# Score chunks made seven ahead from the second block on, and turned-score stores, x stores and v loads issued by GpSimd

## The chip, the cores and the metric

The kernel runs on one core of one Trainium2 chip. The metric is the device time of one execution in microseconds (us), the median of several runs.

## What is computed

Three layers follow each other; B = 4, S = 3072, D = 256, and the inner width of z is 64.

```python
scores = (1.0 / S) * np.matmul(z, z.transpose(0, 2, 1))
attn = np.maximum(scores, 0.0) ** 2
x = u * np.matmul(attn, v)

x_prev = np.concatenate([np.zeros((B, 1, D)), x[:, :-1, :]], axis=1)
xk = mu_k * x + (1.0 - mu_k) * x_prev
xr = mu_r * x + (1.0 - mu_r) * x_prev
k = np.maximum(xk @ w_k, 0.0)
x = 1.0 / (1.0 + np.exp(-(xr @ w_r))) * (k * k @ w_v)

g = np.maximum(x.reshape(B * S, D) @ w_in, 0.0) ** 2
return g @ w_out
```

The change touches the first layer alone, the attention. Its scores are symmetric, since both factors are z.

## The kernel before

The attention of a batch is cut into 6 blocks of 512 queries, 24 blocks in all, numbered here from 0; block `ib` of a batch has 24 **steps**, one for each 128 keys. A step's **chunk** is the 128x512 piece of the squared scores that it needs, split into a high and a low part (`ahi`, `alo`) so that two float32r products stand for one of float32. `attend` (line 406) multiplies the chunk's parts by v's parts (`vhl`), 12 matmuls a step.

A chunk comes about in one of two ways, both in `scores`. For key groups `g >= ib` (a group is 4 chunks) it is computed: six matmuls for two chunks (line 374), relu and square on ScalarE (lines 357 and 378), the high part on ScalarE or VectorE (lines 383 and 381), the low part on VectorE (line 388). For `g > ib` VectorE also turns it (line 335) into a staging tile `turn`, of which there are two; when the group's fourth chunk is in it, the tile is stored to DRAM (`turned`, 1 MB; line 342 in one DMA, or line 340 in four). For `g < ib` the chunk is not computed: the turned piece, stored by an earlier block of the same batch, is loaded into a tile `mixed` (lines 351 and 353) and split (lines 366 and 367).

The program is written in a fixed order, and each engine runs its share in that order. The loop at the end of `attention` goes over the steps. At each it first runs what `at_step` has put there (loads of z, u, v, the turned pieces; the splitting of v and z), then makes the chunks up to step + `ahead`, then does the step's `attend`. `ahead` is 4 in blocks 0 to 2, 5 in block 3, 6 in block 4 and 7 from block 5 on, and it is 0 at a block's steps 21 and 22, in every block, so that no chunk is made there; the chunks left out are made at step 23, behind the block's `gate`. The gate (lines 413 to 429) takes the sums out of PSUM on ScalarE and VectorE, multiplies by u and stores x to DRAM. The next block's sums take the same PSUM banks.

All DMAs but four are issued by SyncE (SP), one after the other; an issue whose wait is not over holds up those behind it. v's loads stand on line 94 (one DMA for a group) or line 288 (four DMAs, groups 2 to 4), eight steps ahead of their splitting. z's second half is copied from its first by a DMA (line 270), which `prep_z` issues 7 steps after z's load; ScalarE takes the high part of the result (line 277) 4 steps after that.

Of the kernel before, what the change touches and what calls it, by code (L numbers as in the profile page):

```python
# [15 lines left out]
P = 128  # L16
Q = 32
T = 512
# [3 lines left out]
def tile_relu2_attention__rwkv_channel_mix__relu2_mlp(  # L22
# [18 lines left out]
    nc = tc.nc  # L41
    B, S, D = u.shape
# [4 lines left out]
    NJ = S // P  # L47
# [7 lines left out]
    G = 4  # L55
# [21 lines left out]
    xT = [dram.tile([D, S], F32, name=f"xT{b}") for b in range(B)]  # L77
    R = P // Q
# [10 lines left out]

    raws = {}  # L90

    def load_raw(key, src, n, w):
        t = raw_p.tile([P, n, w], src.dtype, tag="raw", name="raw")
        nc.sync.dma_start(out=t, in_=src)
        raws[key] = t

    def split_raw(key, hi, lo):
# [139 lines left out]
    def load_piece(i):  # L237
        if i < len(w_pieces):
            src = w_pieces[i][0]
            load_raw(("w32", i), src, src.shape[1], src.shape[2])  # L240

    def attention():
        with ExitStack() as st:
# [3 lines left out]
            FIRST, LEAD = 4, 7  # L247
# [33 lines left out]
            def load_v(b, g):  # L281
                src = v[b, g * T:(g + 1) * T, :]
                if g not in apart:
                    load_raw(("v", b, g), src.rearrange("(c p) d -> p c d", p=P), G, D)
                    return
                raws["v", b, g] = t = raw_p.tile([P, G, D], F32, tag="raw", name="raw")
                for k in range(R):
                    nc.sync.dma_start(out=t[k * Q:(k + 1) * Q], in_=src.rearrange("(r c k) d -> k r c d", r=Q, k=R)[k])

            def hold_v(b, g):  # L290
                vhl[b, g] = zp.tile([P, 2, G, D], F32R, tag="vhl", name="vhl", bufs=NG)
# [39 lines left out]
            def turn(a, i, j, c):  # L331
                if c == 0:
                    staged[i, j] = io.tile([P, R, G, G, Q], F32, tag="turn", name="turn")
                t, s = staged[i, j], spread[i, j]
                nc.vector.transpose(t[:, :, :, c, :], a.rearrange("x (m q r) -> x q m r", m=G, q=R))  # L335
                if c == G - 1:
                    to, src = turned[i, j], t.rearrange("x q m c k -> x q (m c k)")
                    if s:
                        for p in range(R):
                            nc.sync.dma_start(out=to[p].rearrange("q r f -> r q f"), in_=src[p * Q:(p + 1) * Q])  # L340
                    else:
                        nc.sync.dma_start(out=to.rearrange("q x f -> x q f"), in_=src)

            def load_turned_scores(n, g, k):

# [44 lines left out]
            def finish(f=None):  # L390

                if late:
                    late.pop()()
                if f:
                    late.append(f)
# [13 lines left out]
            def gate(n, d):  # L409
                b, t0 = n // NB, (n % NB) * T  # L410
                o, halves = uT.pop((n, d)), acc.pop((n, d))
                part = x_tile[:, d, 0:T] if n < NBLK - 2 else pools["cv"].tile([P, T], F32, tag="em"[d], name="part")
                nc.scalar.copy(part, halves[1])
                if d == 0:
                    rest = io.tile([P, T], F32, tag="rest", name="rest", bufs=1)
                    nc.scalar.copy(rest, halves[0])  # L416
                    spare[n] = rest, part
                    gates.append(lambda: nc.vector.tensor_tensor(out=part, in0=rest, in1=part, op=ALU.add))
                else:
                    nc.vector.tensor_tensor(out=part, in0=halves[0], in1=part, op=ALU.add)  # L420

                def end():
                    to, t_in, u_in = o, part, o
                    if n % NB in apart:
                        to = spare[n][d]
                        t_in, u_in = (t.rearrange("x (k r) -> x k r", r=Q) for t in (t_in, u_in))
                    nc.vector.tensor_tensor(out=to if to is o else to.rearrange("x (r k) -> x k r", r=Q),
                                            in0=t_in, in1=u_in, op=ALU.mult)
                    nc.sync.dma_start(out=xT[b][d * P:(d + 1) * P, t0:t0 + T], in_=to)

                gates.append(end)

# [3 lines left out]
            def at_step(s, f, *a):  # L436
                todo.setdefault(s, []).append((f, a))
# [3 lines left out]
            for n in range(NBLK - 1):  # L441
                b, ib = divmod(n, NB)
                for g in range(ib):
                    need, stored = n * NJ + (g + ib // (NB - 1)) * G - LEAD, (b * NB + g) * NJ + ib * G + G - 1 - FIRST
                    s = max(need - EARLY, stored + 1, freed[-3] if len(freed) > 2 else 0, taken)
                    d = min(3, (need - 3 - s) // 4) or 0.5
# [8 lines left out]
            for b in range(1, B):  # L455
                end = b * NB * NJ
                for g in range(NG):
                    s = end + NJ * (g // 2 - 3) + 6 + 9 * (g % 2)
                    at_step(s, load_z, b, g)
                    for k in range(3):  # L460
                        at_step(s + (7, 11, 13)[k], prep_z, b, g, k)
                    s = end - NJ + G * ((g + 1) % NG) + 5
                    at_step(s - 8, load_v, b, g)
                    for h in range(2):
                        for lo in range(2):
                            at_step(s + 2 * h + lo, prep_v, b, g, h, lo)
# [13 lines left out]
            for n in range(NBLK):  # L480
                s = n * NJ
# [14 lines left out]
            for i, (src, done, rests) in enumerate(conversions):  # L496
                b = i * B // len(conversions)
# [19 lines left out]
            s = n_steps - NJ  # L517
# [11 lines left out]
            for s in range(-FIRST, n_steps + 1):  # L529
                for f, a in todo.pop(s, ()):  # L530
                    f(*a)
                if made == n_steps:
                    finish()
                j = s % NJ if 0 <= s < n_steps else None
                if j in (1, NJ - 1):
                    attend(s, 0, range(3))
                    if j > 1:
                        gate(s // NJ, 0)
                    attend(s - 1, 1, range(3))
                    at.pop(s - 1)  # L540
                    if j > 1:
                        attend(s, 1, range(3))
                        at.pop(s)
                        gate(s // NJ, 1)
                        while gates:
                            gates.pop(0)()
                ahead = 0 if j in (NJ - 3, NJ - 2) else min(LEAD, FIRST + max(0, s - 2 * NJ) // NJ)
                while made < min(n_steps, s + 1 + ahead):
                    scores(made)
                    made += 1  # L550
                if j in (0, NJ - 2):
                    attend(s, 0, range(3))
                elif j == 1:
                    attend(s, 1, range(3))
                    at.pop(s)
                elif j is not None and j < NJ - 2:
                    for d, terms in ((0, (0, 1)), (1, (0, 1)), (0, (2,)), (1, (2,))):
                        attend(s, d, terms)
                    at.pop(s)
# [385 lines left out]
```

## Time and profile before

| what | us |
|---|---|
| median of 3 runs (2543.63 to 2548.68) | 2547.32 |
| the profiled execution, its own time | 2547.61 |
| its span in the profile | 2545.8 |
| attention, to the end of block 23, about | 969 |
| the two layers after it, about | 1577 |

The profile is of one execution. A block of the attention ends, for this document, where VectorE's instruction of line 420 ends; the stretches of the rows below are cut there. The engines are PE (matmul), PEld (weight load), DVE (VectorE), ACT (ScalarE), POOL (GpSimd) and SP, whose issues are marked SPq. "Idle before" names what ended an engine's idle time. A DMA's landing is the time from its issue to its completion.

### The profile page before, as it was taken

The numbers are of one execution on the slowest core, as the hardware profiler recorded it, in microseconds if no ns is written. First come the engines' busy times: TensorE is split into PE (matmuls) and PEld (weight loads), VectorE is DVE, ScalarE is ACT, GpSimd is POOL, SyncE is SP. The second block draws the span as 40 slices with busy tenths as digits, with TensorE's granted clock in tenths as the row PEclk, the third lists the DMA queues.
The fourth block names the chain that finished last, engine by engine and source line by source line (L and its number), as shares of the span: only waits on it lengthen the run. The fifth ranks groups of instructions, "written<-read, shape, count | busy, mean of one in ns | idle before, by whom it ended". The sixth has DMA issues, their size and how long they took to land.

```text
span 2545.8 us, 39407 instructions
## 1 busy us (share of the span) xinstructions
PE 2495.3 (98%) x14832; PEld 2061.4 (81%) x14832; DVE 1988.6 (78%) x3390; ACT 1685.1 (66%) x2943; POOL 0.2 (0%) x4
## 2 busy tenths in 40 slices
PE   7999999999999999999999999999999999999998
PEld 5787788778878878888888888788888888888887
DVE  7777787798878876888888877777777777777776
ACT  7776786697778755555655555666666666666665
POOL 0000000000000000000000000000000000000000
PEclk9999999999999999999999999999999999999999
DMA  8567758767777761212222112011110011010100
GB/s 203 150 165 196 190 160 201 185 189 192 181 194 203 172 176 61 83 63 84 82 71 87 42 67 67 18 26 25 34 34 17 18 34 34 22 29 18 34 17 17
DMA packets 304528, 244.30 MB, mean 96 GB/s; under 512 B 194385, under 2 KB 212817, under 8 KB 304337
## 3 DMA queue, kind: packets, MB, share of 16 engines
q1 hardware_dynamic: 302224, 241.39, 36.1%
q8 instruction: 116, 1.90, 0.3%
q10 hardware_dynamic: 2112, 0.39, 0.1%
q14 instruction: 76, 0.61, 0.1%
HBM read 134.50 MB, written 104.86 MB: 94 GB/s over the span
## 4 chain that ended last, share of the span: by engine, by line
PE 87%; DVE 4%; ACT 3%; DMA 2%; SPq 2%; issue 1%; DVEq 0%; ACTq 0%
PE v L406 25%; PE ups L733 16%; PE ups L208 13%; PE v L749 6%; PE v L750 6%; PE v L751 6%; PE sps L374 4%; PE v L234 3%; PE v L230 3%; PE v L231 3%; DMA mixed<-turned 1%; ACT a L357 1%; ACT a L378 1%; SPq L255 1%; SPq L351 1%
## 5 line engine op out<-in xcount | busy, mean ns | idle before, releaser
L406 PE MATMUL v<-ahi,vhl 64*128 64x512 f32 x4608 | 675.4, 391 | 6.8 <-ACT rest L416 5.5
L406 PEld LDWEIGHTS v<-ahi,vhl 64*128 64x128 f32 x4608 | 472.7, 186 | 97.4 <-ACT rest L416 10.7
L406 PE MATMUL v<-alo,vhl 64*128 64x512 f32 x2304 | 414.0, 392 | 26.0 <-DVE alo L367 18.9
L770 ACT ACTIVATE s<-s 128x512 f32<-128x512 f32 x288 | 181.3, 629 | 333.0 <-DVE s L765 332.9
L733 PE MATMUL ups<-d,win 128*128 128x512 f32 x1152 | 323.6, 389 | 0.0
L406 PEld LDWEIGHTS v<-alo,vhl 64*128 64x128 f32 x2304 | 250.4, 186 | 74.1 <-DVE alo L367 21.9
L749 PE MATMUL v<-hhi,wout 128*128 128x512 f32 x768 | 299.3, 390 | 1.0 <-ACT hhi L778 0.8
L751 PE MATMUL v<-hlo,wout 128*128 128x512 f32 x768 | 299.3, 390 | 0.4 <-DVE hlo L784 0.4
L750 PE MATMUL v<-hhi,wout 128*128 128x512 f32 x768 | 298.8, 389 | 0.0
L208 PE MATMUL ups<-mixed,wk 128*128 128x512 f32 x1152 | 291.8, 389 | 0.0
L784 DVE TENSOR_TENSOR hlo<-s,hhi 128x512 fp32r<-128x512 f32 x384 | 264.6, 689 | 22.2 <-ACT hhi L778 10.8
L160 ACT ACTIVATE a<-ups 128x512 f32<-128x512 f32 x192 | 115.1, 600 | 238.3 <-PE ups L208 231.5
L733 PEld LDWEIGHTS ups<-d,win 128*128 128x128 f32 x1152 | 216.3, 188 | 44.9
L208 PEld LDWEIGHTS ups<-mixed,wk 128*128 128x128 f32 x1152 | 216.2, 188 | 44.9
L733 PE MATMUL ups<-b,win 128*128 128x512 f32 x864 | 242.9, 389 | 0.0
L773 ACT ACTIVATE s<-s 128x512 f32<-128x512 f32 x384 | 231.6, 628 | 6.1
L357 ACT ACTIVATE a<-sps 128x512 f32<-128x512 f32 x336 | 198.6, 591 | 40.3 <-PE sps L374 36.8
L388 DVE TENSOR_TENSOR alo<-a,ahi 128x512 fp32r<-128x512 f32 x336 | 221.0, 661 | 0.0
L378 ACT ACTIVATE a<-a 128x512 f32<-128x512 f32 x336 | 213.1, 634 | 10.2
L335 DVE STREAM_TRANSPOSE turn<-a 128x512 f32<-128x512 f32 x240 | 169.4, 706 | 40.5 <-ACT a L378 35.6
L733 PEld LDWEIGHTS ups<-b,win 128*128 128x128 f32 x864 | 162.0, 188 | 34.2 <-DVE sv L765 0.8
L765 DVE TENSOR_TENSOR s<-ups,su 128x512 f32<-128x512 f32 x192 | 131.2, 683 | 58.8 <-PE ups L733 58.8
(103 smaller groups left out, 3668.0 us busy)
## 6 DMA issues: line engine op xcount, KB each, us to landing
mixed<-turned SPq DMA_DIRECT2D x220, 256.0 KB, 4.8
turned<-turn SPq DMA_DIRECT2D x36, 1024.0 KB, 5.3
turned<-turn SPq DMA_DIRECT2D x96, 256.0 KB, 4.4
u<-in_u_dram SPq DMA_DIRECT2D x192, 64.0 KB, 4.2
x2d<-xo SPq DMA_DIRECT2D x48, 256.0 KB, 2.2
x<-x2d SPq DMA_DIRECT2D x12, 1024.0 KB, 4.8
out_dram<-y SPq DMA_DIRECT2D x94, 128.0 KB, 2.8
x<-xT SPq DMA_DIRECT2D x20, 513.0 KB, 4.1
```

The source lines that it names most:

```text
L208: nc.tensor.matmul(ps, lhsT=lhs(h, c, f), rhs=rhs[:, m, c, :], start=k == 0, stop=k == 3 * ND - 1)
L357: nc.scalar.activation(out=a, in_=ps, func=AF.Relu, scale=1.0 / S)
L378: nc.scalar.activation(out=a, in_=a, func=AF.Square)
L388: finish(lambda: nc.vector.tensor_tensor(out=lo, in0=a, in1=hi, op=ALU.subtract))
L406: nc.tensor.matmul(acc[n, d][i], lhsT=vt[rows, k % 2, c, ds_], rhs=at[s][k // 2][rows], start=first and k == 0, stop=last and k == 2)
L733: nc.tensor.matmul(ps, lhsT=win[q][:, h, r, w], rhs=x(y), start=first and m == 0, stop=m == 2, skip_group_check=not first)
L749: nc.tensor.matmul(acc[p, b][d], lhsT=w[:, 0, c, ds_], rhs=hi, start=first, stop=False)
L750: nc.tensor.matmul(acc[p, b][d], lhsT=w[:, 1, c, ds_], rhs=hi, start=False, stop=False)
L751: nc.tensor.matmul(acc[p, b][d], lhsT=w[:, 0, c, ds_], rhs=lo, start=False, stop=last)
L770: nc.scalar.activation(out=tmp[g, c], in_=banks[g, 0] if c == "11" else tmp[g, c], func=AF.Relu, scale=HS)
L773: nc.scalar.activation(out=tmp[g, c], in_=tmp[g, c], func=AF.Square)
L784: nc.vector.tensor_tensor(out=lo, in0=tmp.pop((g, c)), in1=hi, op=ALU.subtract)
```

## The change

Three things change. `ahead` grows from 4 to 7 in the second block (by one every 6 steps from step 24 on), and steps 21 and 22 make no chunk only where `ahead` has reached 7; so block 0 has no such pause, and blocks 1 to 4 run 7 ahead. The stores of turned scores, the stores of x, v's loads of batches 1 to 3 and those of groups 2 to 4 of batch 0 are issued by GpSimd in place of SP: 237 DMAs (132, 48, 9 and 48). The last two stages of `prep_z` come one step later.

```diff
-    def load_raw(key, src, n, w):
+    def load_raw(key, src, n, w, engine=nc.sync):
         t = raw_p.tile([P, n, w], src.dtype, tag="raw", name="raw")
-        nc.sync.dma_start(out=t, in_=src)
+        engine.dma_start(out=t, in_=src)
...
-                    load_raw(("v", b, g), src.rearrange("(c p) d -> p c d", p=P), G, D)
+                    load_raw(("v", b, g), src.rearrange("(c p) d -> p c d", p=P), G, D, nc.gpsimd if b else nc.sync)
...
-                    nc.sync.dma_start(out=t[k * Q:(k + 1) * Q], in_=src.rearrange("(r c k) d -> k r c d", r=Q, k=R)[k])
+                    nc.gpsimd.dma_start(out=t[k * Q:(k + 1) * Q], in_=src.rearrange("(r c k) d -> k r c d", r=Q, k=R)[k])
...
-                            nc.sync.dma_start(out=to[p].rearrange("q r f -> r q f"), in_=src[p * Q:(p + 1) * Q])
+                            nc.gpsimd.dma_start(out=to[p].rearrange("q r f -> r q f"), in_=src[p * Q:(p + 1) * Q])
                     else:
-                        nc.sync.dma_start(out=to.rearrange("q x f -> x q f"), in_=src)
+                        nc.gpsimd.dma_start(out=to.rearrange("q x f -> x q f"), in_=src)
...
-                    nc.sync.dma_start(out=xT[b][d * P:(d + 1) * P, t0:t0 + T], in_=to)
+                    nc.gpsimd.dma_start(out=xT[b][d * P:(d + 1) * P, t0:t0 + T], in_=to)
...
-                        at_step(s + (7, 11, 13)[k], prep_z, b, g, k)
+                        at_step(s + (7, 12, 14)[k], prep_z, b, g, k)
...
-                ahead = 0 if j in (NJ - 3, NJ - 2) else min(LEAD, FIRST + max(0, s - 2 * NJ) // NJ)
+                ahead = min(LEAD, FIRST + max(0, s - NJ) // 6)
+                if j in (NJ - 3, NJ - 2) and ahead == LEAD:
+                    ahead = 0
```

At the end of block 0, on VectorE, the order changes as follows. Lines 122 to 128 convert a weight, 420 to 427 are the gate, and each instruction of line 367 finishes the low part of a chunk of block 1.

```order
 L122 TENSOR_SCALAR e<-raw 128x512
+L367 TENSOR_TENSOR alo<-mixed,ahi 128x512
 L125 TENSOR_SCALAR e<-e 128x512
+L367 TENSOR_TENSOR alo<-mixed,ahi 128x512
 L128 TENSOR_SCALAR e<-e 128x512
 L420 TENSOR_TENSOR x<-v_264,x 128x512
 L418 TENSOR_TENSOR x<-rest,x 128x512
 L427 TENSOR_TENSOR uT<-x,uT 128x512 x2
-L367 TENSOR_TENSOR alo<-mixed,ahi 128x512 x3
```

The low parts of block 1's first two chunks now stand ahead of the gate; before, all stood behind it.

In block 0, SP held the stores of turned pieces (line 342; the first number is the later block's, 2_94 and 3_96 being those of key groups 2 and 3) between loads. Before:

```order
L342 DMA turned_2_94<-turn 128x4x512
L353 DMA mixed<-turned_1_93 32x4x512
L94 DMA raw<-in_v_dram 128x4x256
L353 DMA mixed<-turned_1_93 32x4x512
L255 DMA u<-in_u_dram 32x16x32 x4
L94 DMA raw<-in_moe_w_k_dram 128x2x512
L342 DMA turned_3_96<-turn 128x4x512
```

On GpSimd's queue after the change, the same stretch:

```order
L288 DMA raw<-in_v_dram 32x4x256 x8
L342 DMA turned_1_93<-turn 128x4x512
L288 DMA raw<-in_v_dram 32x4x256 x4
L342 DMA turned_2_94<-turn 128x4x512
L342 DMA turned_3_96<-turn 128x4x512
L342 DMA turned_4_99<-turn 128x4x512
```

The stores have no loads of u, weights or turned pieces ahead of them any more, only v's loads.

In the last block of batch 0, SP's queue before, from the last loads of turned pieces to the second copy of z (line 270):

```order
L351 DMA mixed<-turned_5_107 128x512 x2
L288 DMA raw<-in_v_dram 32x4x256 x4
L255 DMA u<-in_u_dram 32x16x32 x4
L288 DMA raw<-in_v_dram 32x4x256 x4
L270 DMA zT<-zT 64x512
L255 DMA zn<-in_z_dram 32x16x32 x2
L288 DMA raw<-in_v_dram 32x4x256 x4
```

and after:

```order
L351 DMA mixed<-turned_5_107 128x512 x2
L255 DMA u<-in_u_dram 32x16x32 x4
L270 DMA zT<-zT 64x512
L255 DMA zn<-in_z_dram 32x16x32 x2
L270 DMA zT<-zT 64x512
```

Twelve issues of v's loads have left SP there, eight of them ahead of the copy of z; they stand on GpSimd's queue behind the stores of x of the block before.

## Rows read from the trace of the kernel before

**Rows 1.** The page's first line: the span.

```profile
span 2545.8 us, 39407 instructions
```

**Rows 2.** Stretches: us; PE, PEld, DVE, ACT, POOL busy (count); PE clock; DMA share; GB/s.

```profile
64.80:108.80 44.00, 40.60 (x342) 36.04 (x342) 33.00 (x58) 34.31 (x60) 0.00 (x0) 0.96 0.59 163
108.80:152.30 43.50, 40.06 (x336) 36.64 (x336) 31.43 (x56) 30.70 (x54) 0.00 (x0) 0.96 0.63 160
152.30:195.10 42.80, 39.45 (x330) 36.73 (x330) 32.73 (x58) 27.49 (x49) 0.00 (x0) 0.96 0.70 161
195.10:235.70 40.60, 37.24 (x326) 30.39 (x326) 31.41 (x57) 25.80 (x47) 0.00 (x0) 1.00 0.74 170
235.70:279.00 43.30, 38.14 (x314) 30.00 (x312) 29.43 (x51) 25.05 (x46) 0.00 (x0) 0.96 0.69 171
279.00:319.10 40.10, 39.21 (x339) 31.90 (x341) 36.23 (x66) 34.58 (x62) 0.00 (x0) 1.00 0.81 227
319.10:358.60 39.50, 39.50 (x349) 32.21 (x345) 32.47 (x58) 34.10 (x60) 0.00 (x0) 1.00 0.64 181
358.60:397.00 38.40, 38.40 (x338) 34.39 (x336) 30.42 (x54) 30.19 (x53) 0.00 (x0) 1.00 0.69 173
397.00:434.10 37.10, 37.10 (x326) 30.19 (x324) 30.53 (x54) 26.91 (x48) 0.00 (x0) 1.00 0.82 181
434.10:471.20 37.10, 37.10 (x326) 30.20 (x324) 29.87 (x53) 25.15 (x46) 0.00 (x0) 1.00 0.79 184
471.20:511.10 39.90, 36.28 (x314) 29.05 (x312) 28.60 (x48) 23.94 (x45) 0.00 (x0) 1.00 0.73 186
...
703.20:741.60 38.40, 36.39 (x314) 29.04 (x312) 28.55 (x49) 24.28 (x45) 0.00 (x0) 1.00 0.74 189
...
936.00:2545.00 1609.00, 1601.52 (x7190) 1321.96 (x7188) 1248.13 (x2110) 993.50 (x1729) 0.00 (x0) 1.00 0.16 45
```

**Rows 3.** PE's waits from 0 to 300 us: total, times, longest.

```profile
PE v L406 <- DVE alo L367: 17.3, 5, 4.1
```

**Rows 4.** Timeline at the end of block 2: start, us, instruction.

```profile
154.85 1.88 DVE L367 TENSOR_TENSOR alo<-mixed,ahi 128x512 fp32r<-128x512 f32 x3
...
155.58 0.61 PE L406 MATMUL v<-alo,vhl 64*128 64x512 f32 x2 [4.14 <-DVE alo L367]
```

**Rows 5.** Timeline of DVE and SP in block 0, 39 to 54 us.

```profile
39.53 0.70 DVE L335 STREAM_TRANSPOSE turn<-a 128x512 f32<-128x512 f32 x1
...
46.35 0.41 SPq L342 DMA_DIRECT2D turned<-turn  x1
...
53.29 0.71 DVE L335 STREAM_TRANSPOSE turn<-a 128x512 f32<-128x512 f32 x1 [3.71 <-DMA turned<-turn]
```

**Rows 6.** Stretch 49.0 to 64.1 us, columns as in rows 2.

```profile
49.00:64.10 15.10, 11.12 (x72) 8.67 (x74) 9.11 (x17) 6.84 (x14) 0.00 (x0) 0.77 0.84 279
```

**Rows 7.** ACT's waits from 471 to 512 us, block 11.

```profile
ACT zz L277 <- DMA zT<-zT: 3.5, 1, 3.5
```

**Rows 8.** The tile `turn` from 279 to 320 us: landing of its stores.

```profile
DMA to landing us min/median/max: 4.5/5.3/8.1
```

**Rows 9.** Timeline of DVE in block 6: six of the 20 transposes into `turn`.

```profile
285.74 0.71 DVE L335 STREAM_TRANSPOSE turn<-a 128x512 f32<-128x512 f32 x1
...
292.65 0.72 DVE L335 STREAM_TRANSPOSE turn<-a 128x512 f32<-128x512 f32 x1
293.85 0.71 DVE L335 STREAM_TRANSPOSE turn<-a 128x512 f32<-128x512 f32 x1
...
298.10 0.72 DVE L335 STREAM_TRANSPOSE turn<-a 128x512 f32<-128x512 f32 x1
299.30 0.72 DVE L335 STREAM_TRANSPOSE turn<-a 128x512 f32<-128x512 f32 x1
...
305.66 0.70 DVE L335 STREAM_TRANSPOSE turn<-a 128x512 f32<-128x512 f32 x1
```

**Rows 10.** One of DVE's groups in block 6, 279.0 to 319.1 us: busy us, mean ns, idle before.

```profile
L381 DVE CAST ahi<-a 128x512 fp32r<-128x512 f32 x8 | 3.4, 427 | 0.8 <-ACT a L378 0.8
```

## Prediction

> **What bounds the kernel now.** PE does. I looked first at the busy time by block, since an average over the span hides the blocks. From block 23 on PE is busy 1601.5 of 1609 us, and the change doesn't touch the layers there; they stay as they are. In the attention of batch 1, blocks 7 to 10 have PE busy for their whole length, 39.5, 38.4, 37.1 and 37.1 us, at a granted clock of 1.00. The same four blocks of batch 0 (1 to 4, with the same matmuls) take 44.0, 43.5, 42.8 and 40.6 us, and three of them show a clock of 0.96 [rows 2]. So what can be won lies in batch 0, and a little in the last block of a batch (5, 11, 17), which is longer than PE's work in all three. Everything else of the attention is already at PE's pace.
>
> Then I asked what PE waits for in batch 0: the low part of a loaded chunk, line 367, 17.3 us in 5 waits of up to 4.1 [rows 3]. The timeline at the end of block 2 tells why: VectorE runs that block's gate and only then three low parts in a row, and PE stands for 4.14 us until they come [rows 4]. With 4 chunks of lead and a pause of two steps, too few chunks are ready to cover the gate. With 7 (batch 1) the same gate is covered.
>
> The profiled execution took 2547.61 us with a span of 2545.8 [rows 1], and its own time is 0.3 above the median of 2547.32; I sum against 2547.6. A measurement of this kernel can tell about 0.2% from no change, 5.1 us here.
>
> **The change part by part.**
>
> The *lead*. Blocks 1 to 4 get the order that their likes have in batch 1. PE's work in them is the same; the three further chunks of lead that are built up in block 1 are loaded ones in the end, one high part on ScalarE and one low part on VectorE each, and these two engines are busy 34.3 and 33.0 of block 1's 44.0 us [rows 2], so they hide there. Block 0's missing pause puts two low parts ahead of the gate, which is what PE stood waiting for at the end of block 0. I cost blocks 1 to 4 at their likes: 44.0 - 39.5, 43.5 - 38.4, 42.8 - 37.1 and 40.6 - 37.1, that is 4.5 + 5.1 + 5.7 + 3.5 = **18.8 us gained** [rows 2]. What is late next there is nothing: the likes have no PE idle. If the loads of turned pieces don't keep up with the longer lead, the stalls stay (a rival below).
>
> The *stores on a queue of their own*. In block 0 VectorE wants to write a third staging tile's successor and waits 3.71 us for a store's landing. That store's last transpose began at 39.53, took 0.70, but SP issued the store at 46.35, 6 us late, behind a load of u and one of weights [rows 5]. On GpSimd only v's loads are ahead, and they are out by then. From 40.2 to the wait at 53.29 - 3.71 = 49.6 us there are 9.4 us for a landing. PE is busy 11.12 of 15.10 us between 49.0 and 64.1, at a granted clock of 0.77 [rows 6]: 4.0 idle; a mean of 0.77 means that 46% of the stretch, 6.9 us, ran at 1.2 GHz instead of 2.4, a loss of up to 3.5, part of which falls into the idle time. I take 2.5 of it: **6.5 us gained**, bounds 4.0 and 7.5, and 0 if the landing takes over 9.4. The stores of x are waited for by nothing near.
>
> The *last blocks*. Block 5 takes 43.3, block 11 39.9 us [rows 2]; the difference, **3.4**, I count as won, since block 5 starts from block 4's shorter lead and a queue that had fallen behind. In blocks 11 and 17 there are 39.9 - 36.3 = 3.6 and 38.4 - 36.4 = 2.0 us over PE's work. ScalarE waits 3.5 us for z's copied half there [rows 7]. Eight issues of v leave SP ahead of that copy, and line 277 comes a step later, a step being 37.1 / 24 = 1.5 us [rows 2]. Of that I count 1.4 for each, **2.8**; bounds 0 and 5.6, since the DMA engines are busy 0.73 of block 11 [rows 2] and a second queue makes them no faster. Batch 3 loads no next batch.
>
> The *price of GpSimd*. No row shows a DMA issued by GpSimd, so I bound it. The place where it is tightest is a batch's first block (6, 12, 18): VectorE is busy 36.2 of 40.1 us, a slack of 3.9 [rows 2], it must not wait for a staging tile, and five 1 MB stores are issued. A tile's fourth transpose to the first of the group after next: 285.74 + 0.71 to 293.85, 292.65 + 0.72 to 299.30, 298.10 + 0.72 to 305.66, margins of 7.4, 5.9 and 6.8 us, 20.1 together [rows 9]. SP's stores land in 4.5 to 8.1 us there, 5.3 in the median [rows 8]. At 5.3 a GpSimd store costs nothing. I take the longest, 8.1, as its usual: 3 x 8.1 - 20.1 = 4.2 us of VectorE's time in the block. The second cost: VectorE's casts (8 in such a block, 427 ns each [rows 10]) may have to wait while GpSimd writes descriptors. With seven DMAs a block of X us each, a cast meets one with a chance of 7X / 40.1 and waits X / 2. Nearest rows for X: SP's issue, 0.41 [rows 5], and the landing, 5.3 [rows 8]; between them, at their geometric mean of 1.5, 8 x 0.26 x 0.75 = 1.6 us. Both together 5.8, less the slack 3.9: 1.9 a block, **5.7 us lost** in three blocks. Bounds: 0, and the rivals' prices. Below nothing it can't go, as the gains of the moved issues are counted above. Block 0's margin is 9.4, so it pays none.
>
> The Trainium skill, in "DMA: Bandwidth & Descriptors", section "Latency and other measured facts", gives a first byte after about 1 us for DMAs of GpSimd and 0.6 for SP's. By that the landing would be an estimated 5.7 us, the price nothing and the sum 2516. No row of the kernel before shows it.
>
> The *v loads*. Groups 2 to 4 are four DMAs, wanted every four steps, 6 us [rows 2]; GpSimd has 1.5 us for each. Under that they cost nothing, as they are issued eight steps ahead. At 2.0 each, twelve would be 6 us late in each of blocks 5, 11 and 17, 18 us; I keep that for the range. Behind them on GpSimd stand only x's and the next batch's stores.
>
> **Sum.** 2547.6 - 18.8 - 6.5 - 3.4 - 2.8 + 5.7 = 2521.8; I say **2522 us**.
>
> **The rivals.**
>
> *Late stores (slower than before).* A 1 MB store issued by GpSimd lands late; VectorE stands at line 335 in blocks 6, 12 and 18, and PE with it. Loss per block with a landing of x: 3x - 20.1 + 1.6 - 3.9 = 3x - 22.4. All gains are 31.5 us, so it decides from 3 (3x - 22.4) = 31.5, x = 11, twice the median of SP. At 14 us: 3 x 19.6 = 58.8, time 2547.6 - 31.5 + 58.8 = **2575**. For it: five such stores in 40 us, DMA share already 0.81 [rows 2]; against it: the transfer itself needs 5.3.
>
> *Casts held up.* X of 3 us: 8 x 0.52 x 1.5 = 6.3, with 4.2 for the landing and less 3.9, 6.6 a block, 20 in three: 2547.6 - 31.5 + 20 = **2536**. For it: 8 casts in the tightest block [rows 10]; against it: X would have to be seven times SP's issue of the same store [rows 5]. The Trainium skill, "SBUF — State Buffer", section "Who interferes with whom", states that a VectorE cast in its two-port mode and a GpSimd instruction exclude each other for the whole instruction, whoever comes second being blocked; it speaks against this change, and this rival is what it would do here. No row shows it yet, since GpSimd does nothing.
>
> *The stalls stay.* The lead is written as 7, but the loads of turned pieces, which wait for the stores' landing, don't keep up in batch 0, and PE stands at the block ends as before. Then 18.8 + 3.4 don't come: 2521.8 + 22.2 = **2544**. For it: block 5's lateness even with 7 ahead [rows 2]; against it: the loads' steps were planned for a lead of 7, and batch 1 runs on the same plan without a wait.
>
> **How the numbers follow.** Chances: the forecast 0.56, casts 0.14, stalls stay 0.10, late stores 0.20. Time 2522. The forecast's own bounds: 2547.6 - 18.8 - 7.5 - 7.0 (block 5 down to PE's 36.3) - 5.6 = 2509 without any price, and some 2540 with 18 us of late v loads. The range leaves out the upper half of the late stores and little at the bottom: **2507 to 2562**. Within 0.2% is 2542.2 to 2552.4. Faster: 0.56, 0.09 of the casts, 0.03 of the stalls = 0.68; same: 0.05 + 0.07 = 0.12; slower: 0.20.
>
> **What will show it.** Right: blocks 1 to 4 within half a us of 39.5, 38.4, 37.1 and 37.1; no PE wait of over 2 us at the ends of blocks 0 to 3, and a clock of 1.00 there; line 335 not waiting at 49.6 us; SP's waits for VectorE's transposes gone. Wrong: line 335 waiting for the landing of `turned` in blocks 6, 12 and 18; casts of line 381 longer than 427 ns or late behind GpSimd; ScalarE waiting at line 301 for v; blocks 6 to 10 longer than before, where I expect no change but 1.9 us in block 6.

## The result and the profile after

The changed kernel takes **2514.36 us** in the median of 4 runs (2513.04 to 2514.97), against 2547.32 for the kernel before beside it: a ratio of **0.9873** [0.9854, 0.9892]; the two medians alone give 0.9871. A fourth execution of the kernel before took 4520.09 us and is left out. The profiled execution took 2513.78 us. So 34.0 us of span are gone, where 25.8 were forecast.

The first lines of the page:

```profile
span 2511.8 us, 39719 instructions
...
PE 2486.7 (99%) x14832; PEld 2037.8 (81%) x14832; DVE 1988.4 (79%) x3390; ACT 1681.7 (67%) x2943; POOL 141.9 (6%) x241
```

By stretch, cut as in rows 2 and with its columns: blocks 1 to 6, block 11 and block 17 of the changed kernel.

```profile
61.90:101.30 39.40, 39.40 (x350) 32.18 (x346) 33.33 (x59) 34.40 (x61) 4.35 (x6) 1.00 0.65 183
101.30:139.80 38.50, 38.50 (x338) 31.32 (x336) 31.41 (x56) 30.30 (x54) 7.69 (x14) 1.00 0.69 177
139.80:177.00 37.20, 37.16 (x326) 30.19 (x324) 31.77 (x57) 27.24 (x48) 5.52 (x10) 1.00 0.79 195
177.00:214.10 37.10, 37.03 (x324) 30.19 (x324) 31.15 (x57) 25.13 (x46) 4.26 (x7) 1.00 0.82 203
214.10:250.90 36.80, 35.98 (x314) 29.07 (x312) 28.75 (x48) 23.88 (x45) 9.23 (x16) 1.00 0.72 169
250.90:291.20 40.30, 39.28 (x339) 31.89 (x341) 36.13 (x65) 34.92 (x62) 4.91 (x7) 1.00 0.82 232
443.10:480.40 37.30, 36.04 (x314) 29.07 (x312) 28.68 (x49) 23.77 (x45) 9.23 (x16) 1.00 0.76 179
672.90:709.50 36.60, 35.99 (x314) 29.11 (x316) 28.79 (x48) 23.90 (x45) 9.23 (x16) 1.00 0.75 170
```

Beside rows 2: in blocks 1 to 4 the stretch is as long as PE's busy time, to within 0.1, and the granted clock is 1.00 in all of them. POOL, at nothing before, is busy 4 to 9 us a block, and block 6 is 0.2 us longer than before. Blocks 11 and 17 still have 1.3 and 0.6 us over PE's work.

All that PE waited for from 0 to 300 us, the view of rows 3; the row of line 367 is gone, and what is left of `sps` lies in the first microseconds, but for 1.0 us in block 6:

```profile
PE sps L374 <- DVE zz L279: 8.2, 2, 6.8
PE v L406 <- DVE alo L388: 1.9, 4, 0.9
PE sps L374 <- ACT a L357: 1.0, 1, 1.0
PE v L406 <- ACT rest L416: 0.7, 1, 0.7
PE v L406 <- DVE x L420: 0.2, 1, 0.2
```

The table has the lengths in us, of every kernel's profiled execution. A block's end is the end of VectorE's gate, and that can come up to 2 us earlier or later beside the same PE work. So a batch's last block stands together with the first of the next, and 22 with 23. "Start" is the first matmul of `attend`; it lies in block 0.

| kernel | start | 0 | 1 | 2 | 3 | 4 | 5+6 | 11+12 | 17+18 | 22+23 | median |
|---|---|---|---|---|---|---|---|---|---|---|---|
| before | 11.3 | 64.8 | 44.0 | 43.5 | 42.9 | 40.6 | 83.4 | 80.0 | 78.4 | 72.4 | 2547.3 |
| changed | 13.0 | 61.9 | 39.5 | 38.4 | 37.2 | 37.1 | 77.1 | 77.6 | 76.9 | 70.6 | 2514.4 |
| e1, lead alone | 11.4 | 64.8 | 39.4 | 38.4 | 37.1 | 37.1 | 80.5 | 80.2 | 82.3 | 73.6 | 2529.4 |
| e2, queue alone | 12.6 | 62.0 | 44.2 | 43.5 | 42.9 | 43.2 | 79.1 | 78.7 | 80.0 | 70.5 | 2542.5 |
| e3, v back on SP | 11.5 | 61.9 | 39.4 | 38.5 | 37.1 | 37.1 | 79.2 | 77.4 | 80.5 | 71.0 | 2517.6 |
| e4, all stores back on SP | 13.5 | 64.1 | 39.4 | 38.5 | 37.1 | 37.1 | 75.5 | 75.5 | 75.9 | 73.2 | 2515.1 |
| e5, z's old steps | 13.0 | 62.3 | 39.4 | 38.4 | 37.1 | 37.1 | 78.2 | 78.2 | 80.4 | 70.4 | 2520.8 |
| e6, group 2 back on SP | 11.0 | 60.4 | 39.5 | 38.4 | 37.1 | 37.1 | 76.8 | 79.4 | 80.5 | 70.6 | 2513.3 |
| e7, later landings | 13.3 | 62.2 | 39.5 | 38.4 | 37.1 | 37.1 | 82.8 | 81.7 | 82.1 | 70.5 | 2529.3 |
| e8, pause in block 0 | 13.0 | 62.3 | 43.9 | 38.4 | 37.1 | 37.1 | 77.6 | 77.7 | 77.3 | 70.5 | 2520.0 |
| e9, x back on SP | 13.0 | 62.3 | 39.4 | 38.4 | 37.1 | 37.1 | 76.2 | 75.5 | 75.5 | 70.1 | 2510.5 |
| e10, e9 and e6 | 11.3 | 60.2 | 39.4 | 38.5 | 37.1 | 37.1 | 75.9 | 75.5 | 76.2 | 70.1 | **2508.1** |
| e11, turned back on SP | 13.2 | 63.7 | 39.4 | 38.5 | 37.1 | 38.3 | 76.8 | 77.9 | 76.4 | 72.5 | 2522.4 |

Row by row, changed against before: block 0 lost 2.9 us, blocks 1 to 4 18.7, and the four pairs 6.3, 2.4, 1.6 and 1.8. That is 33.7 of the 34.0. The pairs are also where kernels with the same edits there scatter: "changed" and e6 differ only in block 0's loads, and yet by 1.8 and 3.6 us in 11+12 and 17+18; "before" and e1, alike from block 5 on, differ by 3.9 in 17+18. A difference of under some 4 us in one pair of one profile proves nothing; where a verdict rests on pairs it rests on all three, and on the medians.

### The profile page after: what moved, and what is told of

Read it like the earlier page. It is cut to its first block, busy times and chain, and to the rows that moved or that the text cites. A ratio compares the mean times of both kernels' runs of the same rounds, so it can differ in the third digit from the quotient of the medians.

```text
span 2511.8 us, 39719 instructions
## 1 busy us (share of the span) xinstructions
PE 2486.7 (99%) x14832; PEld 2037.8 (81%) x14832; DVE 1988.4 (79%) x3390; ACT 1681.7 (67%) x2943; POOL 141.9 (6%) x241
## 3 DMA queue, kind: packets, MB, share of 16 engines
q1 hardware_dynamic: 250816, 154.87, 25.8%
## 4 chain that ended last, share of the span: by engine, by line
PE 89%; DVE 5%; ACT 2%; DMA 2%; issue 1%; SPq 0%; DVEq 0%; POOL 0%; ACTq 0%
PE v L406 25%; PE ups L735 17%; PE ups L208 13%; PE v L751 7%; PE v L752 7%; PE v L753 7%; PE sps L374 4%; PE v L234 3%; PE v L230 3%; PE v L231 3%; DMA zn<-in_z_dram 1%; DVE alo L388 1%; DVE turn L335 1%; DVE vhl L299 1%; DMA zT<-zT 1%
## 5 line engine op out<-in xcount | busy, mean ns | idle before, releaser
L406 PE MATMUL v<-ahi,vhl 64*128 64x512 f32 x4608 | 668.4, 388 | 2.9 <-ACT rest L416 2.2
L406 PEld LDWEIGHTS v<-ahi,vhl 64*128 64x128 f32 x4608 | 460.0, 184 | 102.4 <-DVE x L420 7.7
L406 PE MATMUL v<-alo,vhl 64*128 64x512 f32 x2304 | 408.5, 388 | 2.5 <-DVE alo L388 1.9
L406 PEld LDWEIGHTS v<-alo,vhl 64*128 64x128 f32 x2304 | 244.1, 184 | 53.4 <-DVE alo L388 8.6
```

Of the source, the lines that this page charges most:

```text
L406: nc.tensor.matmul(acc[n, d][i], lhsT=vt[rows, k % 2, c, ds_], rhs=at[s][k // 2][rows], start=first and k == 0, stop=last and k == 2)
```

## Experiments

Each is the changed kernel with the edit shown. The ratios are to the kernel before, run beside it; their intervals contain that kernel's own spread, of 5 to 9 us between its fastest and its slowest run. The runs of different experiments are not all from one chip, so medians are compared only where their runs don't overlap.

**The two halves of the change apart.** e1 keeps the lead and issues all from SP at the old steps; e2 keeps GpSimd's issues and has the old lead, and z's old steps. e1 against the changed kernel (the other five DMA lines likewise):

```diff
-                        nc.gpsimd.dma_start(out=to.rearrange("q x f -> x q f"), in_=src)
+                        nc.sync.dma_start(out=to.rearrange("q x f -> x q f"), in_=src)
...
-                        at_step(s + (7, 12, 14)[k], prep_z, b, g, k)
+                        at_step(s + (7, 11, 13)[k], prep_z, b, g, k)
```

> The kernel before with the new rule for `ahead` alone; every DMA stays on SP, and the steps of prep_z are the old ones. Theory (the lead alone ends the stalls at the block ends): blocks 1 to 4 take 39.5, 38.4, 37.2 and 37.1 us as in the changed kernel, 18.7 us less than before, VectorE's wait of 3.7 us for a staging tile in block 0 stays, and the last blocks stay some 3 us longer than in the changed kernel: 2526 us, between 2523 and 2530. Rival (the longer lead needs the stores off SP's queue, since the loads of turned pieces stand behind them): two or more of blocks 1 to 4 stay 2 us or more above these lengths, and the time is 2534 or more.

e2 against the changed kernel:

```diff
-                ahead = min(LEAD, FIRST + max(0, s - NJ) // 6)
-                if j in (NJ - 3, NJ - 2) and ahead == LEAD:
-                    ahead = 0
+                ahead = 0 if j in (NJ - 3, NJ - 2) else min(LEAD, FIRST + max(0, s - 2 * NJ) // NJ)
...
-                        at_step(s + (7, 12, 14)[k], prep_z, b, g, k)
+                        at_step(s + (7, 11, 13)[k], prep_z, b, g, k)
```

> The changed kernel with the old rule for `ahead` and the old steps of prep_z: only the issuing engine of stores and v loads is changed. Theory (the two parts add up): block 0 loses its stall at 50 us, the last blocks and block 22 gain as in the changed kernel, 3 + 4.4 + 2.3 us, the stalls at the ends of blocks 0 to 3 stay at 3 to 4.5 us each: 2535 us, between 2531 and 2540. Rival (what the queue gives is swallowed by the stalls at the block ends, where PE waits anyway): 2543 to 2548.

e1: 2529.42 us, ratio 0.9926 [0.9909, 0.9942]. Blocks 1 to 4 are those of the changed kernel, so the lead alone gives all that is won there, and the loads of turned pieces keep up with SP as their stores' queue as well. Block 0 is as long as before. Timeline of PE in e1 at 50 us, and what VectorE waits for there:

```profile
54.91 1.22 PE L406 MATMUL v<-alo,vhl 64*128 64x512 f32 x4 [3.99 <-DVE alo L388]
```
```profile
DVE turn L335 <- DMA turned<-turn: 4.0, 2, 3.8
```

That is the stall of rows 5, unmoved. e2: 2542.52 us, ratio 0.9976 [0.9967, 0.9986], a miss: it is 2.5 us above the theory's range and just below the rival's. Block 0 loses 2.8, blocks 1 to 3 nothing, and block 4 grows by 2.7, which no run explains. PE's largest row of waits in e2 from 60 to 290 us is the one of rows 3 again:

```profile
PE v L406 <- DVE alo L367: 13.7, 4, 4.1
```

By the ratios e1 is worth 18.9 us and e2 6.1, together 25.0, where the whole change has 32.3 (0.0127 x 2547). Neither has z's later steps; e5 is the change without these.

**z's copy one step later.** e5:

```diff
-                        at_step(s + (7, 12, 14)[k], prep_z, b, g, k)
+                        at_step(s + (7, 11, 13)[k], prep_z, b, g, k)
```

> The changed kernel with the last two stages of prep_z at their old steps, 11 and 13. Theory (the prediction's term of 1.4 us for each of the last blocks): ScalarE waits for z's copied half up to 1.4 us longer in blocks 5, 11 and 17, and the time is 2516 to 2519. Rival (with v's loads off SP the copy lands in time, and what ScalarE waits for there are the turned pieces): no more than 1 us of difference to the changed kernel, 2513 to 2516.

2520.79 us (2519.47 to 2523.13), ratio 0.9885 [0.9865, 0.9906], above both ranges; the pairs are 1.1, 0.6 and 3.5 us longer. What ScalarE waits for in e5 from 440 to 484 us, which holds block 11:

```profile
ACT ahi L366 <- DMA mixed<-turned: 10.0, 2, 5.9
...
ACT zz L277 <- DMA zT<-zT: 1.2, 1, 1.2
```

The last row is the wait of rows 7, come back at 1.2 us; the changed kernel has none for the copied half in its block 11. It stands late in the block, and the gate follows 6.7 us behind it with no other wait of ScalarE between. The other two blocks agree only in part. In block 5 e5 waits 2.0 us for the copied half and the changed kernel 0.4; in block 17 it is 0.3 against the changed kernel's 1.4, and yet 17+18 is the pair that grew most. The runs of the two kernels don't overlap, 6.4 us apart in the median, though the intervals of the ratios do. So the one step is worth some 3 to 6 us, by a mechanism that is seen in blocks 5 and 11 and stays open in block 17; and the lead and the queue without it 29.3: about 4 more than e1 and e2 together. Whether those 4 are a real interaction stays open, since the intervals allow none.

**What pays in block 0's end.** e8 gives block 0 its pause back.

```diff
-                if j in (NJ - 3, NJ - 2) and ahead == LEAD:
+                if j in (NJ - 3, NJ - 2) and True:
```

> The changed kernel with the pause of two steps at the end of block 0 too, where the lead is still 4. Theory (block 0's missing pause is worth the stall of 3.2 us at 64 us and the clock's recovery behind it): PE waits for line 367 behind block 0's gate, block 1 takes 43 to 44 us instead of 39.5, time 2518 to 2519. Rival (the stall came from the late queue in block 0, and stays away without it): block 1 at 39.5 to 40 us, 2514 to 2515.

2520.02 us, ratio 0.9879 [0.9863, 0.9896], 1 us above the theory's range, and 4.4 of the 5.7 us stand in block 1. Timeline of PE at its start:

```profile
61.72 0.39 PE L406 MATMUL v<-ahi,vhl 64*128 64x512 f32 x2
64.91 0.79 PE L406 MATMUL v<-alo,vhl 64*128 64x512 f32 x2 [2.81 <-DVE alo L367]
```

This is rows 4 at the end of block 0: with a lead of 4 and a pause of two steps the gate isn't covered. With the pause gone, two low parts stand ahead of the gate (58.74 and 59.68 us in the changed kernel), and PE waits for none.

**What GpSimd's v loads cost at the start.** In the changed kernel the first `attend` begins 1.7 us later than before. Timelines of VectorE and of GpSimd, to 15 us:

```profile
4.63 0.71 DVE L268 STREAM_TRANSPOSE zT<-zn 128x512 f32<-128x512 f32 x1 [4.63 <-DMA zn<-in_z_dram]
...
8.90 0.71 DVE L268 STREAM_TRANSPOSE zT<-zn 128x512 f32<-128x512 f32 x1 [2.18 <-DMA zn<-in_z_dram]
```
```profile
1.33 2.34 POOL L288 DMA_DIRECT2D raw<-in_v_dram  x4 [0.88 <-POOLq L931]
14.97 2.28 POOL L288 DMA_DIRECT2D raw<-in_v_dram  x4 [11.31 <-DMA zn<-in_z_dram]
```

Nothing holds GpSimd up at 1.33 us, so 512 KB of v for group 2 are asked for while the second tile of z is on its way. On SP they stood behind it. e6 puts these four back:

```diff
-                    nc.gpsimd.dma_start(out=t[k * Q:(k + 1) * Q], in_=src.rearrange("(r c k) d -> k r c d", r=Q, k=R)[k])
+                    (nc.gpsimd if b or g > 2 else nc.sync).dma_start(out=t[k * Q:(k + 1) * Q], in_=src.rearrange("(r c k) d -> k r c d", r=Q, k=R)[k])
```

> The changed kernel with the four v loads of group 2 of batch 0 back on SP; they are the first DMAs that GpSimd issues, at 1.3 us. Theory (they run beside the first loads of z, and delay the second z tile from 6.8 to 8.9 us on VectorE): PE's first attend matmul is 1.7 to 1.9 us earlier, at 11.3 us, and the time 2512.6. Rival (the later start comes from something else, the order of the z loads on SP): the first attend matmul stays at 13.0 us, time 2514.4.

Start at 11.0 us instead of 13.0, block 0 at 60.4 instead of 61.9, and the second transpose waits no more:

```profile
6.92 0.71 DVE L268 STREAM_TRANSPOSE zT<-zn 128x512 f32<-128x512 f32 x1
```

The median, 2513.27 us (2512.99 to 2517.54), ratio 0.9869 [0.9854, 0.9883], isn't told apart from the changed kernel's. e6's profile, of the slowest of its four executions (2517.54), gives the gain back in 11+12 and 17+18, the pairs that scatter. Below, in e10, it shows.

**The price of a late store.** The rival with its point at a landing of 11 us wants a landing of one's own choice. e7 issues eight small stores to a scratch array ahead of each 1 MB store, meant to add some 4.4 us (8 x 0.55) to each; they are extra work.

```diff
+    pads = [dram.tile([P, 16], F32, name=f"pad{k}") for k in range(8)]
...
+                        for k in range(8):
+                            nc.gpsimd.dma_start(out=pads[k], in_=src[:, 0, 0:16])
                         nc.gpsimd.dma_start(out=to.rearrange("q x f -> x q f"), in_=src)
```

> The changed kernel with eight small stores (64 bytes of each of 128 partitions, to a scratch buffer) issued by GpSimd ahead of each 1 MB store of turned scores, which puts the large store 8 x 0.55 = 4.4 us later; its landing, counted from the end of the transposes, goes from 8.1 to 12.5 us in blocks 6, 12 and 18. Theory (the prediction's price for late stores): VectorE waits 3 x 12.5 - 20.1 = 17 us for staging tiles in each of these blocks and has 3.9 us of slack, so each is 13.5 us longer: 2514 + 40 = 2554, more if block 0 pays too. Rival (the seven chunks of lead, 11.7 us of PE's work, take it up and the next block's slack gives it back): these blocks are 3 us longer at most, 2524 or less.

2529.34 us, ratio 0.9928 [0.9908, 0.9948], 15 us above the changed kernel, where my own rule said 40 and its rival 10 at most. But the edit didn't make each store late. Timelines of GpSimd and of VectorE in block 6 of e7 (lines are numbered one higher there):

```profile
255.48 4.44 POOL L344 DMA_DIRECT2D pad<-turn  x8 [0.21 <-issue]
260.42 0.77 POOL L345 DMA_DIRECT2D turned<-turn  x1 [0.49 <-DVE turn L336]
...
273.80 0.54 POOL L344 DMA_DIRECT2D pad<-turn  x1 [1.40 <-DMA turned<-turn]
275.39 0.76 POOL L345 DMA_DIRECT2D turned<-turn  x1 [1.05 <-DVE alo L391]
```
```profile
271.67 0.70 DVE L336 STREAM_TRANSPOSE turn<-a 128x512 f32<-128x512 f32 x1
```

The small stores read what the group's first transpose wrote, so they went out while the tile was still being filled. The first 1 MB store came 0.5 us after its fourth transpose (which ended at 259.90) and the second 0.3, no later than in the changed kernel; the third came 3.0 us after (272.37 to 275.39), its last small store having waited for the landing of the store before, and the fourth 8.5. Landings, counted from the transposes, were 5.4, 7.2, 13.9 and 13.4 us, not 12.5 each. So e7 doesn't test a price for three late stores; it tests what a wait costs. VectorE's waits for staging in blocks 6, 12 and 18 of e7:

```profile
DVE turn L336 <- DMA pad<-turn: 7.2, 1, 7.2
```
```profile
DVE turn L336 <- DMA pad<-turn: 7.5, 2, 5.6
```
```profile
DVE turn L336 <- DMA pad<-turn: 8.6, 2, 5.4
```

Less the slack of 3.9 that is 3.3, 3.6 and 4.7, and these blocks grew by 4.3, 3.4 and 5.0 over the changed kernel's 40.3. So a wait over the slack does lengthen the block, by about what lies over it, and a lead of 7 doesn't absorb it. (The granted clock of e7's block 6 is 0.94, so a part of its growth is PE's own.)

**Which DMAs need to leave SP.** e3 puts v's loads back on SP, e4 all stores (of turned scores and x), e11 only those of turned scores, e9 only those of x. The edits: in e3 (the other line of v's loads likewise)

```diff
-                    nc.gpsimd.dma_start(out=t[k * Q:(k + 1) * Q], in_=src.rearrange("(r c k) d -> k r c d", r=Q, k=R)[k])
+                    nc.sync.dma_start(out=t[k * Q:(k + 1) * Q], in_=src.rearrange("(r c k) d -> k r c d", r=Q, k=R)[k])
```

in e4 and e11 (line 340 likewise)

```diff
-                        nc.gpsimd.dma_start(out=to.rearrange("q x f -> x q f"), in_=src)
+                        nc.sync.dma_start(out=to.rearrange("q x f -> x q f"), in_=src)
```

and in e4 and e9

```diff
-                    nc.gpsimd.dma_start(out=xT[b][d * P:(d + 1) * P, t0:t0 + T], in_=to)
+                    nc.sync.dma_start(out=xT[b][d * P:(d + 1) * P, t0:t0 + T], in_=to)
```

> The changed kernel with all of v's loads back on SP; the stores of turned scores and of x stay on GpSimd. Theory (the stores end the stall at 50 us in block 0, v's loads shorten SP's queue in the last blocks): block 0 ends 1.5 us earlier than in the changed kernel since the start is the old one, blocks 1 to 4 are as there, blocks 5, 11 and 17 are 2 to 3 us longer each, as they have twelve more issues on SP: 2520 us, between 2517 and 2524. Rival (v's loads gain nothing by leaving SP, since the DMA engines are what is busy in the last blocks): 2513 or less, the start's 1.5 us below the changed kernel.

2517.64 us (2515.66 to 2519.97), ratio 0.987 [0.9853, 0.9888]: within the theory's range, its runs above all of the changed kernel's, and not told apart from it by the ratio. The terms didn't come as expected: `attend` starts at 11.5 us and yet block 0 ends no earlier, and 5+6 and 17+18 are 2.1 and 3.6 us longer, 11+12 is not.

> The changed kernel with the stores of turned scores and of x back on SP; v's loads stay on GpSimd. Theory: VectorE waits for a staging tile in block 0 again, 3.7 us, and block 0 and 1 together are 5 to 6 us longer; block 22 is 2.3 us longer, as its last loads of turned pieces stand behind the last stores again; blocks 6, 12 and 18 are 0.2 us shorter: 2521 us, between 2518 and 2525. Rival (the stores' move is worth nothing once v's loads are off SP and the lead is 7): 2514 to 2516.

2515.14 us (2514.15 to 2517.03), ratio 0.9861 [0.9844, 0.9878]. A miss: six us better than expected. It lies in the rival's range, but the rival's reason, that the stores' move is worth nothing, doesn't hold: block 0 has its stall again and 22+23 are 73.2, yet the three pairs are down to 75.5, 75.5 and 75.9, the shortest of all. So something in the changed kernel's last blocks was being lost, and it came with the stores. GpSimd's timeline around the end of block 10, of the changed kernel (block 10 ends at 443.1):

```profile
436.90 0.77 POOL L94 DMA_DIRECT2D raw<-in_v_dram  x1
445.42 0.56 POOL L429 DMA_DIRECT2D xT<-rest  x1 [7.74 <-ACT ahi L366]
446.27 0.56 POOL L429 DMA_DIRECT2D xT<-x  x1 [0.29 <-DVE x L427]
447.00 1.51 POOL L94 DMA_DIRECT2D raw<-in_v_dram  x2 [0.17 <-issue]
```

Two loads of v stand behind two stores of x that wait for the gate, and come out 10 us after the first. The theory formed on this: x's stores hold up v's loads, and v then collides with the loads of turned pieces. e9 and e11 tell it from its rival, that the stores of turned scores do.

> The changed kernel with the stores of x alone back on SP. On GpSimd's queue v's loads of groups 0 and 1 then no longer stand behind the x stores of the fifth block, which wait for its gate. Theory (those two loads, 1 MB issued at 447 us in one burst beside the loads of turned pieces, are what ScalarE's waits in the last blocks come from): they are issued about 10 us earlier, blocks 5, 11 and 17 take 35 to 36.3 us instead of 36.8, 37.3 and 36.6, the rest stays: 2510 us, between 2507 and 2512. Rival (it is the turned stores' leaving GpSimd that shortened these blocks where all stores were on SP): they stay at 36.5 to 37.5, time 2513 to 2516, or more where SP's loads wait behind the x stores.

> The changed kernel with the stores of turned scores alone back on SP; x's stores and v's loads stay on GpSimd. Theory: block 0 ends 2 us later and block 22 takes 39.9 instead of 37.1 us, since loads of turned pieces stand behind stores on SP again, and the last blocks stay as in the changed kernel, since v's loads of groups 0 and 1 still stand behind the x stores: 2519 us, between 2517 and 2522. Rival (the turned stores' leaving GpSimd shortens the last blocks): these take 34.5 to 35.6 us, time 2514 to 2516.

e9: **2510.52** us (2509.22 to 2513.0), ratio 0.9853 [0.9834, 0.9871]; its pairs 76.2, 75.5 and 75.5, 4.3 us below the changed kernel's in all. e11: 2522.36 us, ratio 0.9894 [0.9876, 0.9911]; its pairs, 76.8, 77.9 and 76.4, are no shorter than the changed kernel's. It lies just above its range: block 4 is 1.2 us longer and 22+23 1.8, and so are blocks 10 and 16, by 1.9 and 0.7, which no run explains. So x it was; three pairs of kernels say so that differ in x's stores alone, and in each the one with x on SP is faster with no overlap of the runs: e9 against the changed kernel by 3.8 us in the median, e10 (below) against e6 by 5.2, e4 against e11 by 7.2. GpSimd's timeline in e9, where block 10 ends at 442.6:

```profile
435.71 1.52 POOL L94 DMA_DIRECT2D raw<-in_v_dram  x2
438.34 0.76 POOL L94 DMA_DIRECT2D raw<-in_v_dram  x1 [1.12 <-issue]
```

And SP's last loads of turned pieces in block 11, of the changed kernel and of e9:

```profile
452.95 4.15 SPq L351 DMA_DIRECT2D mixed<-turned  x4
...
458.50 1.04 SPq L351 DMA_DIRECT2D mixed<-turned  x2
```
```profile
451.63 1.86 SPq L351 DMA_DIRECT2D mixed<-turned  x4
...
454.88 1.04 SPq L351 DMA_DIRECT2D mixed<-turned  x2
```

They are out 3.1 us sooner after the block's start (458.50 - 443.1 = 15.4, against 454.88 - 442.6 = 12.3), and four issues take 1.86 us instead of 4.15. PE in e9's block 11 has no idle time:

```profile
442.60:477.50 34.90, 34.90 (x308) 28.78 (x308) 28.62 (x49) 23.39 (x44) 6.62 (x12) 1.00 0.78 188
```

Where v's loads come out, and that x's stores decide it, is shown; that they slow the issues of turned pieces by their traffic is read from times that agree, and no run isolates it.

**Both together.** e10 is e9 with e6's edit.

> The changed kernel with the stores of x and the v loads of group 2 of batch 0 on SP: on GpSimd remain the stores of turned scores and v's other loads. Theory: the start of 11.0 us and a block 0 of 60.4 as where only group 2 went back, 1.5 us less, and the shorter last blocks: 2508.5 us, between 2505 and 2511, below the changed kernel's 2514.4. Rival: the last blocks vary by 2 to 3 us from run to run whatever is done, and the time is 2513.

**2508.06** us (2506.95 to 2508.62), ratio 0.9839 [0.9824, 0.9854], 6.3 us below the changed kernel and 2.5 below e9 on the same chip, with no overlap of the runs. Here the start's 1.7 us show. It is the fastest of all.

## Why the prediction was right, and where not

The direction, the range and the largest term held. The time came out 7.7 us below the forecast, from terms wrong in both directions. By the spans, in the prediction's order:

**The lead.** Forecast 18.8, measured 18.7, and e1 gives the same with nothing else changed. Costing each block at its like in the next batch was exact, because the order of work became the same. Two things carry it, and e8 parts them: with block 0's pause kept, block 1 takes 43.9 us, while blocks 2 to 4 need only the 7. The rival "the stalls stay" is out.

**Block 0.** Forecast 6.5, measured 2.9. The step on the stall held: VectorE's transposes wait for nothing at 50 us, and from the start of `attend` to the end block 0 went from 53.5 to 48.9 us, 4.6 less (the bounds were 4.0 and 7.5). These are the two stretches, before and changed, with the columns of rows 2:

```profile
11.30:64.80 53.50, 47.26 (x355) 34.94 (x351) 45.45 (x82) 42.20 (x77) 0.00 (x0) 0.94 0.78 207
```
```profile
13.00:61.90 48.90, 46.42 (x359) 34.94 (x357) 46.33 (x84) 43.07 (x79) 8.26 (x13) 1.00 0.88 224
```

PE's idle time fell from 6.2 to 2.5 us, near the 4.0 forecast, and its busy time by 0.8: the 2.5 that I took for the clock was mis-sized, though the granted clock did rise from 0.94 to 1.00. Two short waits for line 388, 1.1 us together, are what is late next. What I missed is the other end: "on GpSimd only v's loads are ahead, and they are out by then" is right at 40 us, and these same loads cost 1.7 us at 1.3 us. They had been priced as late loads only, never as early ones that delay z.

**The last blocks.** Forecast 3.4 + 1.4 + 1.4 = 6.2 and bounds that allow more; blocks 5, 11 and 17 became 6.5, 2.6 and 1.8 shorter, 10.9. Block 5's part was put down to block 4's short lead and to the queue, and both bear on it: 5+6 is 2.9 us shorter than before in e1 and 4.3 in e2, each near the scatter of a pair. The mechanism for blocks 11 and 17, ScalarE no longer waiting for z's copied half [rows 7], holds in block 11, where e5 brings the wait back. For block 17 it isn't shown: the changed kernel still waits 1.4 us there. Nor does such a wait cost its length everywhere: e9 has 2.1 us of it early in block 11, and no idle PE. The later step gave some 3 to 6 us over three blocks, where 1.4 for each of two was counted. Taking v's loads off SP, the other half of that reason, gave between nothing, by e3's ratio, and some 3, by its median. And I wrote that behind v's loads on GpSimd "stand only x's and the next batch's stores"; the order that matters is the reverse. v's loads stand behind x's, whose wait for the gate delays them by 10 us, and this cost some 4 us of what was to be had (e9).

**The price of GpSimd.** Forecast 5.7 (1.9 in each of three blocks), measured 0.2 a block. The usual landing was sized well: I took 8.1 us, and the tile `turn` shows it in block 6, from a store's issue:

```profile
DMA to landing us min/median/max: 4.8/8.0/9.0
```

(8.1 and 8.6 in the median in blocks 12 and 18.) Over the whole kernel the page has 7.3 for the 1 MB stores, where SP's had 5.3:

```profile
turned<-turn POOLq DMA_DIRECT2D x36, 1024.0 KB, 7.3
```

From the landing on, the term was too large twice. First the wait. VectorE's transposes in block 6, the last of the third group, and the first of the fourth and of the fifth:

```profile
270.04 0.71 DVE L335 STREAM_TRANSPOSE turn<-a 128x512 f32<-128x512 f32 x1
274.16 0.71 DVE L335 STREAM_TRANSPOSE turn<-a 128x512 f32<-128x512 f32 x1 [2.85 <-DMA turned<-turn]
...
279.88 0.70 DVE L335 STREAM_TRANSPOSE turn<-a 128x512 f32<-128x512 f32 x1
```

One wait of 2.8 us instead of 4.2 (3.1 and 2.8 in the other two blocks). The sum took three landings of 8.1 against three margins of their old size [rows 9]. The first store landed in 4.8 us and cost nothing. The second, issued 0.4 us after its last transpose, took 9.0 and made the wait. That wait pushed the next transposes back, so the third store's margin was 9.1 us (270.04 + 0.71 to 279.88) in place of 6.8, and its landing of 8.0 stayed within it. Second the casts: X is 0.56 to 0.76 us, not 1.5, as GpSimd's rows of the whole kernel have it (busy us, mean ns, idle before), and a cast in block 6 is in the mean as long as before [rows 10]:

```profile
L340 POOL DMA_DIRECT2D turned<-turn x96 | 53.4, 563 | 274.6 <-DVE turn L335 250.5 <-DMA mixed<-turned 23.2 <-issue 0.7
L342 POOL DMA_DIRECT2D turned<-turn x36 | 27.3, 758 | 230.7 <-DVE turn L335 173.8 <-DMA mixed<-turned 46.2 <-DMA u<-in_u_dram 10.7
```
```profile
L381 DVE CAST ahi<-a 128x512 fp32r<-128x512 f32 x8 | 3.3, 418 | 0.0
```

2.8 of wait is under the slack of 3.9, and the block pays 0.2. So one of the prediction's signs of being wrong, line 335 waiting in these blocks, is there and costs next to nothing. That slack rule is the part of the step that e7 confirms. Both priced rivals, late stores and casts held up, are out, the first because 8 us isn't 11.

On the two pages: the Trainium skill, "DMA: Bandwidth & Descriptors", section "Latency and other measured facts", has GpSimd's DMAs begin later, by which I estimated a landing of 5.7 us. The trace has 8.0 in these blocks, and it decides. Its estimate of the price, nothing, is closer than mine, but by the slack and not by the landing. With the rule of the Trainium skill, "SBUF — State Buffer", section "Who interferes with whom", the trace agrees in a small part. Of the changed kernel's 168 casts of line 381, 21 overlap a DMA issue of GpSimd; three of these took 0.54, 0.66 and 0.54 us, while the other 18, and the 147 that overlap none, took at most 0.43, as did all 168 before the change. The longest stands beside the issue of 436.90 shown above:

```profile
437.25 0.66 DVE L381 CAST ahi<-a 128x512 fp32r<-128x512 f32 x1
```

Together the three cost some 0.5 us in the whole attention. Whether these casts run in the two-port mode that the rule is about, no run shows.

**v's loads** were forecast at nothing, and at 18 us for the range if GpSimd took 2.0 us for each; it takes 0.56. Their times of issue mattered, too early at the start and too late in the last blocks, and their lengths did not.

**Not in the sum.** 22+23 became 1.8 us shorter. They stay long in e1, e4 and e11, whose turned scores are stored by SP, and are short wherever GpSimd stores them, so those stores on SP cost it; that they hold up the last loads of turned pieces there, as ScalarE's waits suggest, no run isolates. I had looked at the last blocks of three batches and called the fourth free, as it loads no next batch.

In all, against the forecast of 25.8 us of gain: 3.6 less in block 0, 4.7 more in the last blocks, 5.1 more from the price, 1.8 from 22+23, which makes 33.8, and 34.0 were measured. Errors of that size in terms that were bounded from far rows are no surprise. That the total came as near as 8 us is partly luck, since block 0's error stands against the others. It was the lead, which could be read from a like block, that decided the sign.

## What to carry to other kernels

Where the same block occurs with and without a stall in one trace, cost the change by the difference of the two; it was exact here to 0.1 us. When DMAs go to a second queue, ask of each what now stands ahead of it: a store that waits for compute delays every load behind it (x ahead of v, 4 us), and a load with nothing ahead of it starts so early that it delays a more urgent one (1.7 us at the start). A wait for a buffer that is late also moves the buffer's later uses, so waits along one rotation of buffers are walked through in order, not added up. And look in the trace whether an edit that is to delay a transfer did delay it: extra DMAs that wait for less than the transfer does run ahead of it (e7).

## What the runs showed of the hardware

A DMA issued by GpSimd keeps it busy for 0.56 us (256 KB of a turned piece, or a quarter of a group of v) to 0.76 (1 MB, or a whole group of v), and of VectorE's 21 casts that overlap such an issue three took 0.54 to 0.66 us where others take 0.43 at most. A 1 MB store takes 7.3 us to land in the median, against 5.3 in e11, where SP issues it and the rest is the same, and a 256 KB one 4.8 against 4.4. With x's stores off GpSimd (e9) the 7.3 become 6.2. SP's issues aren't of fixed length either: four loads of turned pieces took 1.86 us or 4.15 in the same place of the program, the longer with v's loads coming out within the 6 us before.
